# Later pairs' q and k by way of DRAM scratch, transposed as float32r, and the order ranked anew

## Chip, core and metric

The kernel runs on one core of a Trainium2 chip. The metric is the device time of one execution in microseconds (us), smaller is better. TensorE (PE, with its weight loads as PEld), VectorE (DVE), ScalarE (ACT), GpSimd (POOL) and SyncE (SP, which here only issues DMAs) each work through an instruction list of their own in order and meet at semaphores. TensorE multiplies a moving operand with a stationary one, which a weight load has put into the array before, and writes to PSUM. A tile is a buffer in SBUF or PSUM, the two memories on the chip.

## The reference

Attention with a compressive memory over 4 batches of 8 heads (576 tokens, width 64), then two feed-forward blocks on its output as 2304 tokens of width 512:

```python
scores = scale * np.matmul(q, k.transpose(0, 1, 3, 2))      # causal mask, softmax -> a
local = np.matmul(a, v)
q_p = phi(q)                                                # elu(q) + 1
mem_out = einsum(q_p, M_prev) / (einsum(q_p, z_prev) + 1e-6)
x = g * mem_out + (1 - g) * local                           # g = sigmoid(beta), per head
r = np.maximum(x @ w_in, 0.0)                               # 512 -> 2048
x = (s * (r * r) + b) @ w_out                               # 2048 -> 512
out = (sigmoid(x @ w_gate) * (x @ w_val)) @ w_out2          # 512 -> 1536 -> 512
```

## The kernel before

**Stages.** The 32 heads are taken as 16 pairs of heads, numbered j = 0 to 15, four to a batch. Attention fills about the first 390 us. The product with w_in (tiles `h`, line 338; 128 chunks of twelve multiplications, `h_2_0_5` is chunk 5 of the first window of batch 2) can begin for a batch when its four pairs are done, and its chunks stand between the attention of the following pairs. Then come y (the product with w_out, line 1555, which reads r back from DRAM), the products m with w_gate and w_val (line 1874) and o with w_out2 (line 2008).

**A pair.** q and k come in as [128 tokens, 5 blocks, 2 x 64] (`rawq`, `rawk`, two buffers each). Both are needed with the width on the partitions, so TensorE turns each of the five 128x128 blocks: `transposed` (line 467) makes a block the stationary operand and multiplies it with an identity matrix (tiles `qt`, `kt`). ScalarE and VectorE write the result to SBUF as two float32r tiles, a rounded part and its rest (`QT`, `KT`). Next come scores (`sc`), softmax (VectorE's `nm`, ScalarE's exponentials `P`), turned probabilities (`pt`), and the product with v (`acc`). The first batch's four pairs (`DIRECT`, j = 0 to 3) take another way with float32 products (`o`, `ret`, `xt`), the twelve later ones keep all products in float32r. In the later pairs GpSimd normalises the probabilities (line 778) before they are turned, and `ft` turns phi(q). The profile prints f32 for float32r operands of TensorE too; which they are is seen in the code: `KT`, `QT`, `PTB`, `PT_A`, `VHL`, `x`, `w_in` are float32r, `rawq`, `rawk`, `ident`, `phi` and `P` are float32.

**Order.** A planner (`Plan`) writes every engine's list. Each step has an engine, a cost, an urgency worked out from the table `TUNE`, and what it reads, writes and needs as buffers; `order` simulates them and takes the most urgent step that is ready. The table and the costs thus change nothing but the order; on the chip every list is followed as it stands, on SP too.

## Time and profile before

| | |
|---|---|
| median of 3 runs | 1046.77 us (1042.32 to 1053.78) |
| the profiled execution | 1041.78 us, of which its span (first to last instruction) is 1040.0 us |
| granted TensorE clock, mean of the span | 0.997 |
| TensorE busy | 1018.5 us, 98% |
| VectorE, ScalarE, GpSimd busy | 827.9, 602.4, 174.0 us |
| DMA | 230.60 MB, mean 222 GB/s |

Busy times of TensorE count a multiplication from its start to its modelled end, and neighbours overlap. So what a multiplication takes from TensorE's time is read from the distance of two starts, not from its own length, and a wait is read where the timeline names a releaser.

### The profile page before, as it was taken

How to read it: one execution, taken by the hardware profiler on the slowest of the kernel's cores; microseconds unless marked ns; L12 is line 12 of the kernel's file. 1: busy time of each engine (PE TensorE's matmuls, PEld its weight loads, DVE VectorE, ACT ScalarE, POOL GpSimd, SP SyncE). 2: the span in 40 equal slices, each digit the busy share in tenths (PEclk: the TensorE clock that was granted, in tenths of full speed). 3: DMA queues.
4: the chain of work that ended last, by engine and by line, in shares of the span. 5: the costliest groups of instructions: out<-in, count | busy, mean ns of one | idle time of the engine just before them, and what ended most of it. 6: DMA issues, size and time to landing. Idle time of an engine off the chain costs nothing.

```text
span 1040.0 us, 20327 instructions
## 1 busy us (share of the span) xinstructions
PE 1018.5 (98%) x7182; PEld 991.5 (95%) x7182; DVE 827.9 (80%) x1760; ACT 602.4 (58%) x1322; POOL 174.0 (17%) x258
## 2 busy tenths in 40 slices
PE   6999999999999999999999999999999999999998
PEld 4888999999999999999999999999999999999998
DVE  5888888987887766788998884878968779677775
ACT  5778787877787667666877674223531226322243
POOL 2345655444444420000000000000000000000000
PEclk9999999999999999999999999999999999999999
DMA  6634454344534239877989988777797778877774
GB/s 139 152 101 114 138 144 131 100 127 119 147 116 129 92 135 337 286 253 278 324 290 364 375 301 300 248 254 253 265 347 256 254 257 263 282 267 251 253 268 157
DMA packets 182885, 230.60 MB, mean 222 GB/s; under 512 B 71936, under 2 KB 136960, under 8 KB 182784
## 3 DMA queue, kind: packets, MB, share of 16 engines
q1 hardware_dynamic: 181136, 228.48, 67.2%
q8 instruction: 57, 0.93, 0.4%
q10 hardware_dynamic: 1648, 0.82, 0.3%
q14 instruction: 44, 0.36, 0.1%
HBM read 171.06 MB, written 58.20 MB: 220 GB/s over the span
## 4 chain that ended last, share of the span: by engine, by line
PE 95%; DMA 1%; DVE 1%; ACT 1%; issue 1%; SPq 0%; POOL 0%; ACTq 0%; DVEq 0%; POOLq 0%
PE m L1874 25%; PE y L1555 19%; PE h L338 19%; PE o L2008 13%; PE sc L720 3%; PE acc L904 2%; PE o L1283 2%; PE acc L905 2%; PE pt_B L851 1%; PE sc L746 1%; PE acc L908 1%; PE pt_D L851 1%; PE pt_A L851 1%; PE sc L1150 1%; PE ft L467 1%; PE qt L467 1%
## 5 line engine op out<-in xcount | busy, mean ns | idle before, releaser
L1874 PE MATMUL m<-yt,ws 128*128 128x384 f32 x1512 | 262.6, 335 | 0.0
L1874 PEld LDWEIGHTS m<-yt,ws 128*128 128x128 f32 x1512 | 262.0, 188 | 0.0
L338 PE MATMUL h<-x,w_in 128*128 128x256 f32 (+1 forms) x1536 | 224.7, 300 | 2.1 <-ACT r L348 2.0
L338 PEld LDWEIGHTS h<-x,w_in 128*128 128x128 f32 x1536 | 209.2, 190 | 5.2 <-ACT r L348 2.7
L1886 DVE TENSOR_TENSOR set<-m,set 128x384 f32<-128x384 f32 x252 | 132.6, 553 | 53.4 <-PE m L1874 47.8
L1555 PE MATMUL y<-gh,w_out 128*128 128x384 f32 (+1 forms) x768 | 150.5, 338 | 0.0
L1555 PEld LDWEIGHTS y<-gh,w_out 128*128 128x128 f32 x768 | 135.5, 188 | 0.0
L2008 PE MATMUL o<-wo,ps 128*128 128x256 f32 x1134 | 134.0, 280 | 0.0
L2008 PEld LDWEIGHTS o<-wo,ps 128*128 128x128 f32 x1134 | 133.9, 188 | 0.0
L1890 ACT ACTIVATE set<-set 128x384 f32<-128x384 f32 x72 | 37.9, 526 | 84.6 <-DVE set L1886 84.6
L348 ACT ACTIVATE r<-h 128x320 f32<-128x320 f32 (+1 forms) x128 | 52.0, 410 | 57.3 <-PE h L338 51.3
L1555 PE MATMUL y<-gl,w_out 128*128 128x384 f32 x384 | 83.0, 337 | 0.0
L1990 ACT CAST ps<-p 128x384 fp32r<-128x384 f32 x72 | 36.9, 513 | 68.7 <-PE o L2008 35.1
L700 DVE CUSTOM_DVE_ANT_0 P<-sc,mask 128x256 f32<-128x256 f32 (+4 forms) x144 | 68.1, 514 | 8.2 <-PE sc L720 5.6
L1555 PEld LDWEIGHTS y<-gl,w_out 128*128 128x128 f32 x384 | 68.6, 188 | 0.0
L778 POOL TENSOR_SCALAR P<-P,rs 128x384 f32<-128x384 f32 (+4 forms) x108 | 64.5, 618 | 20.2 <-DVE rs L774 17.1
L762 ACT ACTIVATE P<-P,nm 128x384 f32<-128x384 f32 (+4 forms) x108 | 62.4, 580 | 9.1 <-DVE nm L700 8.7
L1540 DVE TENSOR_TENSOR gl<-rr,gh 128x384 fp32r<-128x384 f32 x96 | 52.6, 555 | 14.1 <-PE y L1555 6.7
L1535 ACT CAST gh<-rr 128x384 fp32r<-128x384 f32 (+1 forms) x96 | 49.1, 512 | 18.7 <-PE y L1555 14.6
L1882 ACT COPY set<-m 128x384 f32<-128x384 f32 x36 | 17.4, 482 | 72.0 <-PE m L1874 72.0
L1531 ACT ACTIVATE rr<-rr 128x384 f32<-128x384 f32 (+1 forms) x96 | 49.0, 521 | 3.0 <-DMA rr<-relu_scratch 2.8
L1994 DVE TENSOR_TENSOR ps<-p,ps 128x384 fp32r<-128x384 f32 x72 | 39.8, 555 | 11.4 <-ACT ps L1990 9.9
(194 smaller groups left out, 1583.9 us busy)
## 6 DMA issues: line engine op xcount, KB each, us to landing
ws<-weight_scratch SPq DMA_DIRECT2D x108, 512.0 KB, 4.6
wo<-out_weight_scratch SPq DMA_DIRECT2D x63, 512.0 KB, 4.3
rr<-relu_scratch SPq DMA_DIRECT2D x96, 192.0 KB, 5.0
weight_scratch<-wp SPq DMA_DIRECT2D x36, 512.0 KB, 5.5
out_weight_scratch<-ov_h SPq DMA_DIRECT2D x42, 256.0 KB, 3.4
relu_scratch<-r SPq DMA_DIRECT2D x32, 320.0 KB, 2.6
ws<-weight_scratch SPq DMA_DIRECT2D x36, 256.0 KB, 3.2
raw_w_in<-in_moe_w_in_dram SPq DMA_DIRECT2D x16, 512.0 KB, 4.4
```

Of the source, the lines that this page charges most:

```text
L338: nc.tensor.matmul(t[:, :n], wt[:, wi, c], x[:, xi, c], start=(m == 0), stop=(m == 3 * NK - 1))
L348: nc.scalar.activation(rts[b, c0, f - f % 2][:, f % 2, :n], t[:, :n], AF.Relu)
L700: nc.vector.tensor_tensor_reduce(out=pr, in0=ps, in1=mk, scale=1.0, scalar=3e38, op0=ALU.add, op1=ALU.min, accum_out=nm,)
L762: nc.scalar.activation(pr, pr, AF.Exp, bias=T.pop(("nm", j, e, t)), scale=-1.0, accum_out=T["sums", j][:, col : col + 1],)
L778: nc.gpsimd.tensor_scalar(out=pr, in0=pr, scalar1=T["rs", j, part][:, n : n + 1], scalar2=1.0, op0=ALU.mult, op1=ALU.mult,)
L1531: nc.scalar.activation(r_sb[step], r_sb[step], AF.Square)
L1535: nc.scalar.copy(gh, r_sb[step])
L1540: nc.vector.tensor_tensor(out=gl, in0=r_sb.pop(step)[:, :n], in1=gs[step][0][:, :n].bitcast(F32), op=ALU.subtract,)
L1555: nc.tensor.matmul(accs[wi][d][:, : y.shape[1]], w_out_sb[f][:, x, d], y, start=(f == 0 and x == 0 and y is gh), stop=(f == NF - 1 and y i ...
L1874: nc.tensor.matmul(acc, wt[:, a, k : k + P], yt[:, y, c], start=(m == 0), stop=(m == 3 * K2 - 1),)
L1886: nc.vector.tensor_tensor(out=t[:, o], in0=Z["m", z, x], in1=t[:, i], op=ALU.add)
L2008: nc.tensor.matmul(Z["zo", pi, x, i][:, c * C : (c + 1) * C], ps[:, a, r * P : (r + 1) * P], wt[:, y * C : (y + 1) * C], start=(f == 0 and ...
```

## The change

Four things are changed. For the twelve later pairs, SP first copies the pair's q and k, DRAM to DRAM, into scratch tensors of its own (`copy`: 24 copies of 288 KB), and the loads read the scratch. The tiles they fill are float32r (written through a float32 view, so that the words are not converted), and `transposed` then multiplies with an identity of type float32r. The first four pairs keep float32. The identity is made in a buffer of another tile and copied over by GpSimd. The planner reckons 58 ns in place of 112 ns for a block in all `qt` and `kt`, gets the 24 copies as steps, and has a new table, so the order of nearly everything up to the end of the attention is another; from the last chunks of `h` to the end TensorE's list is the same instruction by instruction.

```diff
--- before.py
+++ after.py
-    "mem": -104539.7, "lq": 25883.4, "lk": -1533.8, "lv": 53002.6, "lm": 1567.6, "q": -1758.6,
...
+    "mem": -106340.2, "lq": 27443.5, "lk": -1029.3, "lv": 41230.5, "lm": 1427.5, "q": -1937.4,
...
+    qs_d = dram("q_scratch", [B, H, S, D])
+    ks_d = dram("k_scratch", [B, H, S, D])
...
-    ident = const.tile([P, P], F32, name="ident")
-    nc.gpsimd.memset(ident, 0.0)
+    identr = const.tile([P, P], F32R, name="identr")
+    ident = identr.bitcast(F32)
+    eye = stage.tile([P, NK * P], F32, tag="f", name="eye", bufs=FB)[:, :P]
...
+    nc.gpsimd.tensor_copy(identr, eye)
...
-    rawqs = [at.tile([P, NQ, P], F32, name=f"rawq{i}", bufs=1) for i in range(2)]
-    rawks = [at.tile([P, NQ, P], F32, name=f"rawk{i}", bufs=1) for i in range(2)]
     rawv = at.tile([P, NQ, P], F32, name="rawv", bufs=1)
+    raws = {}
+
+    def raw_of(c, j):
+        return raws[c, j % 2, j in DIRECT]
+
+    def make_raw(j):
+        for c in "qk":
+            t = raws[c, j % 2, j in DIRECT] = at.tile(
+                [P, NQ, P], F32 if j in DIRECT else F32R, tag=f"raw{c}{j % 2}", name=f"raw{c}{j}",
+                bufs=1,
+            )
+            t = t if j in DIRECT else t.bitcast(F32)
+            if c == "k":
+                nc.gpsimd.memset(t[LAST:, NQ - 1], 0.0)
+                continue
+            for e in range(2):
+                r = slice(e * LAST, (e + 1) * LAST)
+                nc.gpsimd.memset(t[r, NQ - 1, (1 - e) * D : (2 - e) * D], 0.0)
...
+        from_q, from_k = src is q, src is k
+        if from_q or from_k:
+            dst = raw_of("q" if from_q else "k", j)
+            if j not in DIRECT:
+                dst, src = dst.bitcast(F32), qs_d if from_q else ks_d
...
+    def copy(j, src):
+        b, p = jobs[j][:2]
+        h = slice(2 * p, 2 * p + 2)
+        nc.sync.dma_start((qs_d if src is q else ks_d)[b, h], src[b, h])
...
-            nc.tensor.transpose(o, src[:, i], ident)
+            if src.dtype == F32R:
+                nc.tensor.transpose(o.bitcast(F32R), src[:, i], identr)
+            else:
+                nc.tensor.transpose(o, src[:, i], ident)
...
+            bounce = not direct and src is not v
+            if bounce:
+                add(
+                    "SP", 450, lambda src=src: copy(j, src), u + du + AT["cp"],
+                    reads=[("ld", j - 2)], writes=[(key + "d", j)], late=2300, size=3e5,
+                )
             add(
                 "ACT" if src is q and j == 0 else "SP", 600 * ne,
                 lambda src=src, dst=dst, ta=ta: load_raw(j, src, dst, ta), u + du,
-                new=[(key, (key, j))], late=2300, size=(t1 - ta) * P * (500 if direct else 800),
+                reads=[(key + "d", j)] if bounce else [],
+                writes=([(key, j)] if first and src is not v else []) + ([("ld", j)] if src is k else []),
+                new=[] if first and src is not v else [(key, (key, j))], late=2300, size=(t1 - ta) * P * (500 if direct else 800),
...
-        add("PE", flip(nt), qt, u + AT["q"], reads=[("rawq", j)],
+        add("PE", 58 * nt + 30, qt, u + AT["q"], reads=[("rawq", j)],
```

The start of the program on SP, before and changed (`raw_w_in` is a part of w_in, `mem` of M_prev and z_prev; the number behind a name is the pair, or the part of w_in):

```order
L410 DMA rawk0_93<-in_k_dram 128x4x64 x2
L421 DMA rawk0_93<-in_k_dram 64x2x64
L410 DMA rawk1_94<-in_k_dram 128x4x64 x2
L421 DMA rawk1_94<-in_k_dram 64x2x64
L251 DMA raw_w_in0_136<-in_moe_w_in_dram 128x4x256
L251 DMA raw_w_in1_142<-in_moe_w_in_dram 128x4x256
L448 DMA mem0_147<-in_M_prev_dram 128x64
L449 DMA mem0_147<-in_z_prev_dram 128x1
```

```order
L256 DMA raw_w_in0_111<-in_moe_w_in_dram 128x4x256
L256 DMA raw_w_in1_114<-in_moe_w_in_dram 128x4x256
L473 DMA mem0_117<-in_M_prev_dram 128x64
L474 DMA mem0_117<-in_z_prev_dram 128x1
L430 DMA rawk0_102<-in_k_dram 128x4x64 x2
L441 DMA rawk0_102<-in_k_dram 64x2x64
L430 DMA rawk1_107<-in_k_dram 128x4x64 x2
L441 DMA rawk1_107<-in_k_dram 64x2x64
```

The first two parts of w_in and pair 0's memory now stand ahead of k of pairs 0 and 1.

The start of the program on TensorE, before and changed:

```order
L467 MATMUL kt0_154<-ident_64,rawk0_93 128x128 x5
L467 MATMUL qt0_0_167<-ident_64,rawq0_91 128x128 x4
L467 MATMUL qt0_4_172<-ident_64,rawq0_91 128x128
L467 MATMUL kt1_188<-ident_64,rawk1_94 128x128 x5
L1150 MATMUL sc0_0_0_203<-KT0_165,QT0_185 128x128
L1150 MATMUL sc0_1_0_204<-KT0_165,QT0_185 128x128
...
L1095 MATMUL ret0_0_229<-mem0_147,phi0_194 128x65
```

```order
L495 MATMUL qt0_0_180<-identr_64,rawq0_99 128x128 x4
L495 MATMUL qt0_4_185<-identr_64,rawq0_99 128x128
L495 MATMUL kt0_190<-identr_64,rawk0_102 128x128 x5
L1138 MATMUL ret0_0_226<-mem0_117,phi0_203 128x65
L1138 MATMUL ret0_1_227<-mem0_117,phi0_203 128x65
...
L1144 MATMUL ret0_0_226<-mem0_117,phi0_203 64x65 x2
L495 MATMUL kt1_241<-identr_64,rawk1_107 128x128 x5
L1193 MATMUL sc0_0_0_258<-KT0_210,QT0_196 128x128
L1193 MATMUL sc0_1_0_259<-KT0_210,QT0_196 128x128
```

The scores of pair 0 (`sc0`) now stand behind its memory product (`ret0`), and q's transposes ahead of k's.

TensorE where pair 4 follows pair 3, before and changed (`qt6` and `ft4` are transposes of pairs 6 and 4, `xt3` turns pair 3's output, `pt4_B0` and `pt4_A0` turn normalised probabilities of pair 4):

```order
L467 MATMUL qt6_1321<-ident_64,rawq0_91 128x128 x5
L1317 MATMUL xt3_1_1348<-ident_64,X3_1_1309 128x128 x2
L1324 MATMUL xt3_1_1348<-ident_64,X3_1_1309 64x64 x2
L467 MATMUL ft4_1357<-ident_64,phi4_1037 128x128 x5
L338 MATMUL h_0_256_0_1375<-x0_256_770,w_in0_138 128x320 x12
L851 MATMUL pt4_A0_1398<-ident_64,P4_0_0_1318 128x128
L851 MATMUL pt4_A0_1398<-ident_64,P4_0_1_1328 128x128 x2
L851 MATMUL pt4_B0_1402<-ident_64,P4_4_1288 128x128
L851 MATMUL pt4_B0_1402<-ident_64,P4_0_2_1223 128x128
```

```order
L493 MATMUL qt6_1367<-identr_64,rawq4_505 128x128 x5
L1360 MATMUL xt3_1_1395<-identr_64,X3_1_1361 128x128 x2
L1367 MATMUL xt3_1_1395<-identr_64,X3_1_1361 64x64 x2
L495 MATMUL ft4_1402<-identr_64,phi4_1015 128x128 x5
L894 MATMUL pt4_B0_1428<-identr_64,P4_4_1339 128x128
L894 MATMUL pt4_B0_1428<-identr_64,P4_0_2_1291 128x128
L894 MATMUL pt4_B0_1428<-identr_64,P4_0_3_1322 128x128
...
L894 MATMUL pt4_A0_1457<-identr_64,P4_0_0_1374 128x128
L894 MATMUL pt4_A0_1457<-identr_64,P4_0_1_1377 128x128 x2
L343 MATMUL h_0_256_0_1465<-x0_256_836,w_in0_113 128x320 x12
```

The chunk of `h` that stood between `ft4` and the first `pt4` now stands behind all of them.

TensorE at the end of the attention, before and changed (`acc15_0_1` is the last product that x of the first window of batch 3, `x3_0`, waits for):

```order
L338 MATMUL h_2_256_15_5760<-x2_256_4548,w_in15_2315 128x320 x12
L904 MATMUL acc15_0_1_5778<-PT15_A1_5758,VHL15_5229 128x256
...
L908 MATMUL acc15_0_1_5778<-FS15_1_5596,mst15_5222 128x256
L851 MATMUL pt15_D1_5785<-ident_64,P15_1_3_5536 128x128
...
L904 MATMUL acc15_1_0_5789<-PTB15_5691,VHL15_5229 128x320
...
L908 MATMUL acc15_1_0_5789<-FS15_0_5595,mst15_5222 128x320
L904 MATMUL acc15_1_1_5807<-PTB15_5691,VHL15_5229 128x320
...
L338 MATMUL h_3_0_0_5825<-x3_0_5805,w_in0_138 128x256 x12
```

```order
L343 MATMUL h_2_256_15_5789<-x2_256_4685,w_in15_2017 128x320 x12
L947 MATMUL acc15_0_0_5809<-PT15_A0_5786,VHL15_5341 128x256
...
L894 MATMUL pt15_D1_5839<-identr_64,P15_1_3_5648 128x128
...
L947 MATMUL acc15_1_0_5844<-PTB15_5775,VHL15_5341 128x320
...
L951 MATMUL acc15_1_0_5844<-FS15_0_5751,mst15_5332 128x320
L947 MATMUL acc15_0_1_5861<-PT15_A1_5836,VHL15_5341 128x256
...
L951 MATMUL acc15_0_1_5861<-FS15_1_5752,mst15_5332 128x256
L947 MATMUL acc15_1_1_5870<-PTB15_5775,VHL15_5341 128x320
...
L343 MATMUL h_3_0_0_5895<-x3_0_5886,w_in0_113 128x256 x12
```

`acc15_0_1` is moved behind `acc15_1_0`, so that only `acc15_1_1` stands between it and the chunk `h_3_0_0`, which reads `x3_0`.

## Rows read from the trace of the kernel before

**Rows 1.** The page: busy us by engine (share of the span, instructions), and the chain.
```profile
PE 1018.5 (98%) x7182; PEld 991.5 (95%) x7182; DVE 827.9 (80%) x1760; ACT 602.4 (58%) x1322; POOL 174.0 (17%) x258
...
PE 95%; DMA 1%; DVE 1%; ACT 1%; issue 1%; SPq 0%; POOL 0%; ACTq 0%; DVEq 0%; POOLq 0%
```

**Rows 2.** One stretch: us, busy us by engine (instructions), granted clock, DMA share, GB/s.
```profile
320.00:360.00 40.00, 40.00 (x310) 38.02 (x309) 31.33 (x74) 27.38 (x70) 14.65 (x18) 1.00 0.33 109
```

**Rows 3.** Group of TensorE multiplications: count, busy us, mean ns, idle before.
```profile
L467 PE MATMUL kt<-ident,rawk 128*128 128x128 f32 x80 | 12.7, 294 | 6.0 <-DMA rawk<-in_k_dram 5.5 <-DVE KT L1072 0.5
```

**Rows 4.** Groups of TensorE weight loads (PEld), columns as in rows 3.
```profile
L904 PEld LDWEIGHTS acc<-PTB,VHL 128*128 128x128 f32 x96 | 18.1, 188 | 2.8 <-DVE nm L700 0.7 <-issue 0.6
...
L905 PEld LDWEIGHTS acc<-PTB,VHL 128*64 128x64 f32 x96 | 13.1, 136 | 0.0
...
L467 PEld LDWEIGHTS kt<-ident,rawk 128*128 128x128 f32 x80 | 9.8, 150 | 7.0 <-POOL vals L440 5.5 <-DVE KT L1072 0.9 <-PE pt_A L851 0.3
```

**Rows 5.** Timeline: first and fifth transpose of a later pair's k (start, us, engine, line).
```profile
321.71 0.27 PE L467 MATMUL kt<-ident,rawk 128*128 128x128 f32 x1
...
322.14 0.27 PE L467 MATMUL kt<-ident,rawk 128*128 128x128 f32 x1
```

**Rows 6.** Timeline, three products of a later pair, one behind the other on TensorE.
```profile
207.42 0.22 PE L904 MATMUL acc<-PT_A,VHL 128*128 128x128 f32 x1
207.48 0.22 PE L905 MATMUL acc<-PT_A,VHL 128*64 128x128 f32 x1
...
207.54 0.33 PE L908 MATMUL acc<-FS,mst 128*128 128x256 f32 x1
```

**Rows 7.** Timeline of the first 27 us, TensorE and ScalarE.
```profile
5.48 1.34 PE L467 MATMUL kt<-ident,rawk 128*128 128x128 f32 x5 [5.48 <-DMA rawk<-in_k_dram]
...
9.61 1.65 PE L1150 MATMUL sc<-KT,QT 64*128 64x128 f32 x12
...
10.33 0.68 ACT L269 ACTIVATE f_w_in<-raw_w_in 128x512 f32<-128x512 f32 x1
...
17.21 0.48 ACT L1260 COPY PT_A<-pt_A 128x384 f32<-128x384 f32 x1 [4.32 <-PE pt_A L1243]
...
26.25 1.23 ACT L287 CAST w_in<-raw_w_in 128x512 fp32r<-128x512 f32 x2
```

**Rows 8.** Waits of TensorE, the second to fifth longest of 13: total us, times, longest.
```profile
PE h L338 <- ACT r L348: 2.0, 1, 2.0
PE xt L1317 <- POOL X L1309: 1.7, 1, 1.7
PE pt_C L1243 <- ACT P L1190: 1.4, 1, 1.4
PE ret L1095 <- DMA mem<-in_z_prev_dram: 1.2, 1, 1.2
```

**Rows 9.** Timeline at 91 us, GpSimd and TensorE, where pair 4 follows pair 3.
```profile
91.25 4.80 POOL L778 TENSOR_SCALAR P<-P,rs 128x384 f32<-128x384 f32 x9 [0.39 <-DVE rs L774]
...
92.07 3.06 PE L338 MATMUL h<-x,w_in 128*128 128x320 f32 x12
```

**Rows 10.** Group of GpSimd: normalisation of one block of probabilities, 512 columns.
```profile
L778 POOL TENSOR_SCALAR P<-P,rs 128x512 f32<-128x512 f32 x24 | 17.8, 741 | 0.0
```

**Rows 11.** Timeline at 381 us, from the attention's last products to h.
```profile
380.87 0.37 ACT L928 COPY XB<-acc 64x256 f32<-64x256 f32 x1
...
382.29 0.31 PE L904 MATMUL acc<-PTB,VHL 128*128 128x320 f32 x1
...
382.80 1.22 DVE L996 TENSOR_TENSOR x<-XB,x 128x1024 fp32r<-128x1024 f32 x1 [0.66 <-ACT x L992]
...
383.69 2.57 PE L338 MATMUL h<-x,w_in 128*128 128x256 f32 x18
```

**Rows 12.** DMA issues: out<-in, engine, count, KB each, median us to landing.
```profile
ws<-weight_scratch SPq DMA_DIRECT2D x108, 512.0 KB, 4.6
...
rawk<-in_k_dram SPq DMA_DIRECT2D x32, 128.0 KB, 3.0
```

More of the change, by code (lines that the diff above doesn't have):

```diff
@@ L209, in attention_moe_kernel @@
     w1 = w1s.enter_context(tc.tile_pool(name="w1", bufs=16, side="left"))
-    ident = const.tile([P, P], F32, name="ident")
-    nc.gpsimd.memset(ident, 0.0)
+    identr = const.tile([P, P], F32R, name="identr")
+    ident = identr.bitcast(F32)
+    eye = stage.tile([P, NK * P], F32, tag="f", name="eye", bufs=FB)[:, :P]
+    nc.gpsimd.memset(eye, 0.0)
     nc.gpsimd.affine_select(
-        out=ident, in_=ident, compare_op=ALU.not_equal, fill=1.0, base=0,
+        out=eye, in_=eye, compare_op=ALU.not_equal, fill=1.0, base=0,
         pattern=[[-1, P]], channel_multiplier=1,
     )
+    nc.gpsimd.tensor_copy(identr, eye)
     gt = const.tile([P, H], F32, name="gt")
@@ L355, in h_store @@
         )
-    rawqs = [at.tile([P, NQ, P], F32, name=f"rawq{i}", bufs=1) for i in range(2)]
-    rawks = [at.tile([P, NQ, P], F32, name=f"rawk{i}", bufs=1) for i in range(2)]
     rawv = at.tile([P, NQ, P], F32, name="rawv", bufs=1)
-    def zero_raw():
-        for t in rawks:
-            nc.gpsimd.memset(t[LAST:, NQ - 1], 0.0)
-        for t in rawqs:
-            for e in range(2):
-                nc.gpsimd.memset(t[e * LAST : (e + 1) * LAST, NQ - 1, (1 - e) * D : (2 - e) * D], 0.0)
+    raws = {}
[14 more added lines that the diff above has]
+                nc.gpsimd.memset(t[r, NQ - 1, (1 - e) * D : (2 - e) * D], 0.0)
+    def zero_raw():
+        make_raw(0)
+        make_raw(1)
         nc.gpsimd.memset(rawv[: P - LAST, NQ - 1], 0.0)
@@ L413, in load_raw @@
             )
-        if t1 == NQ and src is q:
+        if t1 == NQ and from_q:
             for e in range(2):
@@ L419, in load_raw @@
         elif t1 == NQ:
-            lo = 0 if src is k else P - LAST
+            lo = 0 if from_k else P - LAST
             eng.dma_start(
@@ L529, in plan_load @@
         direct = j in DIRECT
+        first = j in (0, 1, NP, NP + 1)
+        if j in (NP, NP + 1):
+            add("POOL", 900, lambda: make_raw(j), u + AT["lq"] - 20,
+                new=[("rawq", ("rawq", j)), ("rawk", ("rawk", j))])
+        elif first:
+            add("BAR", 0, lambda: None, -1000, reads=[("zero", 0)],
+                new=[("rawq", ("rawq", j)), ("rawk", ("rawk", j))], late=0)
         for src, dst, ta, key, du in (
-            (q, rawqs[j % 2], t0, "rawq", AT["lq"]), (k, rawks[j % 2], 0, "rawk", AT["lk"]),
+            (q, None, t0, "rawq", AT["lq"]), (k, None, 0, "rawk", AT["lk"]),
             (v, rawv, 0, "rawv", AT["lv"]),
@@ L563, in qt @@
         def qt():
-            T["qt", j] = transposed(rawqs[j % 2], t0, t1, f"qt{j}")
+            T["qt", j] = transposed(raw_of("q", j), t0, t1, f"qt{j}")
         def q_hi():
@@ L583, in kt @@
         def kt():
-            T["kt", j] = transposed(rawks[j % 2], 0, t1, f"kt{j}")[:, :nk]
+            T["kt", j] = transposed(raw_of("k", j), 0, t1, f"kt{j}")[:, :nk]
         def k_hi():
@@ L594, in k_lo @@
             )
-        add("PE", flip(t1), kt, u + AT["k"], reads=[("rawk", j)],
+        add("PE", 58 * t1 + 30, kt, u + AT["k"], reads=[("rawk", j)],
             new=[(bank(t1), ("kt", j)), ("KT", ("KT", j))], late=250)
@@ L607, in phi_a @@
             nc.scalar.activation(
-                flat(), rawqs[j % 2][:, t0:t1].rearrange("p t d -> p (t d)"), AF.Relu, scale=-1.0
+                flat(), raw_of("q", j)[:, t0:t1].rearrange("p t d -> p (t d)").bitcast(F32), AF.Relu, scale=-1.0
             )
@@ L613, in phi_b @@
             nc.vector.scalar_tensor_tensor(
-                out=flat(), in0=rawqs[j % 2][:, t0:t1].rearrange("p t d -> p (t d)"), scalar=0.0,
+                out=flat(), in0=raw_of("q", j)[:, t0:t1].rearrange("p t d -> p (t d)").bitcast(F32), scalar=0.0,
                 in1=flat(), op0=ALU.max, op1=ALU.add,
@@ L1017, in qt @@
             T["qt", j] = [
-                (slice(a * P, c * P), transposed(rawqs[j % 2], a, c, f"qt{j}_{a}", True)) for a, c in parts
+                (slice(a * P, c * P), transposed(raw_of("q", j), a, c, f"qt{j}_{a}", True)) for a, c in parts
             ]
@@ L1063, in kt @@
         def kt():
-            T["kt", j] = transposed(rawks[j % 2], 0, t1, f"kt{j}", True)[:, :nk]
+            T["kt", j] = transposed(raw_of("k", j), 0, t1, f"kt{j}", True)[:, :nk]
         def k_hi():
@@ L2110, in attention_moe_kernel @@
     AT = TUNE
+    add("POOL", 1500, zero_raw, -1000, writes=[("zero", 0)])
     add("ACT", 500, load_consts, AT["lc"], writes=[("gates", 0)], late=2300, size=4e3)
```

1 line of the change is left out of this document (removed), and 14 rows, old and new, of the table TUNE.

## Prediction

> **What bounds the kernel now.** I read the page's busy table and its chain first. TensorE is busy for 1018.5 of 1040.0 us, and the chain that ended last lies on it for 95%; no other engine has more than 1% of that chain [rows 1]. The one-stretch view says the same of the middle of the attention: in 320 to 360 us TensorE works all 40 us, and the DMA engines stand at a share of 0.33 [rows 2]. So a nanosecond of TensorE saved there counts nearly whole, provided that its list has something ready to move up. In the attention that something is `h`: its chunks stand between the steps of every pair from the fifth on. A nanosecond taken from another engine counts nothing, except where TensorE is seen to wait. TensorE's waits are few. The longest is the first one, 5.5 us for k of pair 0 [rows 3], and the next four are 2.0, 1.7, 1.4 and 1.2 us long, each once [rows 8]. From the last chunks of `h` on, TensorE's order is unchanged, so whatever is won or lost by then is carried to the end.
>
> **Term 1, the transposes.** The first of five transposes of a later pair's k begins at 321.71 and the fifth at 322.14 us [rows 5]: four distances in 0.43 us, 0.108 us each. What would they take as float32r? The nearest rows are products with a float32r moving operand of 128 columns, as the identity will be: they begin at 207.42, 207.48 and the next at 207.54 us, 60 ns apart [rows 6]. TensorE has 80 such products for all `kt`, five in each of 16 pairs [rows 3], and as many for `qt`; the twelve later pairs have 120 of the 160. So 120 x (108 - 60) ns = 5.8 us. The other end is nothing: what may hold a row of transposes back is the weight load, because each transpose loads a block of its own. A float32r load of 128 columns stands in the trace with 188 ns and one of 64 columns with 136 ns, while the float32 blocks of k took 150 ns [rows 4]. The 64 columns more cost 52 ns, and if they cost that in every row, 128 columns take 104 ns, and a chain of float32r transposes keeps the distance that it has. Against it: between 207.42 and 207.54 us the loads of 64 and of 128 columns both went in, in 0.12 us [rows 6], where that price gives 156 ns. I take -5.8, with 0 as the other end.
>
> The Trainium skill has a rule that speaks against the change: its page "TensorE: Matmul & The Clock Gate", section "LDWEIGHTS (loading the stationary operand)", puts a load at its columns over 1.2 in ns, whatever else, which is 107 ns for 128 columns, an estimate almost equal to the present distance; by it term 1 would be about 0. The trace disagrees for pairs of loads (0.12 us where the rule gives 160 ns) [rows 6], so I give it no more than the chance of its rival below. The same page's section "Weight-path perf modes" says that a faster load is taken for 128 weights whose type is not FP32; float32r's longer load rows [rows 4] do not show it.
>
> **Term 2, the start.** Two parts of w_in, 512 KB each, and pair 0's memory now stand ahead of k on SP. On ScalarE two passes over w_in and one cast stand ahead of the evictions of `qt0`, 0.68 + 0.68 us and half of 1.23 us [rows 7], 2.0 us. On TensorE `sc0`, twelve products in 1.65 us, and pair 1's `kt`, 1.34 us like the first one [rows 7], leave the place where they ran beside the wait for the memory and go behind it. If none of that is made good, it costs 1.65 + 1.34 = 3.0 us. For it speaks that this work has to be done at some time: today the cast stands at 26.25 us, in the way of pair 0's softmax, ScalarE has 4.32 us idle before 17.21 us [rows 7], and TensorE waits 1.4 us for P and 1.2 us for the memory [rows 8], which now lands earlier. If both waits go, and half of the idle time is put to use besides, about 2 us are won on balance. I take +0.5, near the middle, with -2 and +3 as ends.
>
> **Term 3, pair 3 to pair 4.** Today a chunk of `h` of 3.06 us begins right behind `ft4` at 92.07 us [rows 9] and gives GpSimd time to normalise pair 4's probabilities. In the changed list `pt4_B0` stands right behind `ft4` and needs three normalised blocks. GpSimd begins them at 91.25 us [rows 9], at up to 0.74 us a block [rows 10]: 91.25 + 2.2 = 93.4 us against 92.07, a new wait of 1.3 us. It is nothing if GpSimd begins earlier by as much, and at most the 3.06 us that the chunk has covered. I take +1.3, ends 0 and +3.
>
> **Term 4, the end of the attention.** `x3_0` needs `acc15_0_1`. From its first eviction at 380.87 us to the end of the last step on VectorE, at 382.80 + 1.22 = 384.02 us, it takes 3.15 us [rows 11]. In the changed list only `acc15_1_1` and the first two products of `h_3_0_0` (which read the half of x that is ready sooner) stand in between: 383.69 - 382.29 = 1.4 us for the one [rows 11] and, by 2.57 us for 18 products, 2 x 0.14 us for the others. That leaves 1.5 us of waiting. Today a later chunk of the same batch waits 2.0 us for ScalarE's r [rows 8]; a delay ahead of it shortens that wait, and I credit somewhat more than half. So +0.6, ends 0 and +1.5.
>
> **Parts taken at nothing.** The 24 copies of 288 KB lie between the 128 KB loads, 3.0 us from issue to landing, and the 512 KB ones, 4.6 us [rows 12]. In the changed SP list a copy stands some fifteen entries or more ahead of the load that reads it; DMA engines at a share of 0.33 [rows 2] can take what is added. If a copy came late, the load would stop SP, and with it the stores of r behind it: that is the third rival. The identity's way by a second buffer, and its copy on GpSimd, lie beside the first wait of 5.5 us [rows 3]. The planner's lower cost is only an order, in the terms above.
>
> **The sum.** -5.8 + 0.5 + 1.3 + 0.6 = -3.4 us. The profiled execution took 1041.78 us, 1.8 us more than its span of 1040.0, so it would take 1038.4. The median of the three runs shown is 5.0 us above the profiled one, and the same sum from there is 1046.77 - 3.4 = 1043.4. I predict 1043 us. With every end against the forecast but term 1's the sum is -5.8 + 3 + 3 + 1.5 = +1.7 (1048.5), with every end for it -5.8 - 2 = -7.8 (1039.0).
>
> **Rivals.** *The transposes don't get faster.* The load of a new block every time sets the pace at 104 ns, as the 52 ns for 64 columns say [rows 4]. Then only the new waits are left, +2.4 us, 1049.2. For it: those load rows, longer for float32r than for float32. Against it: the distances of 60 ns [rows 6].
>
> *The order wins too.* The new table removes waits that I leave in place: the four of 2.0, 1.7, 1.4 and 1.2 us make 6.3 us [rows 8]. If they go, and the new places cost nothing, -5.8 - 6.3 = -12.1 us, 1034.7. For it: nearly everything ahead of 390 us is ordered afresh. Against it: in the two places that I followed I count new waits.
>
> *Slower: the copies hold up SP.* Every entry of SP's list waits for those ahead of it. If a copy lands later than the entries between it and its load have been issued, the load stops the list, stores of r stand, the buffers of r stay full, and the next chunk of `h` cannot be evicted. By the 18 products in 2.57 us [rows 11] a chunk of twelve takes 1.7 us; one lost in each of the twelve later pairs is 20.6 us, and with the sum of -3.4 it gives +17.2, 1064. It decides once a copy takes several times the 4.6 us of a 512 KB transfer [rows 12]. Against it: the DMA share of 0.33 [rows 2], and that the copies run about two pairs ahead.
>
> **How the numbers follow.** My forecast has a chance of 0.59, the unchanged transposes 0.20, the better order 0.13, the held-up SP 0.08. A change of 1% (10.5 us) is about what a measurement of this kernel can tell from no change. Faster by over 1% is below 1036.3: the better order and little else, 0.15. Slower by over 1% is above 1057.2: the held-up SP, 0.08. The rest, 0.77, is within 1%. The range of 1034 to 1051 takes in the forecast's ends (1039.0 to 1048.5), the unchanged transposes (1049.2) and the better order (1034.7), and leaves out the held-up SP and some of the spread of the runs.
>
> **What would show it.** The distances of `kt` and `qt` transposes in later pairs: 60 ns right, 104 or more wrong. In the timeline: the start of the first `sc` (9.61 us before [rows 7]); the wait of `pt_B` for GpSimd near 92 us, 1.3 us; the wait of `h` for VectorE's x near 382 us, 1.5 us. In the view of waits no raw load of a later pair should hold TensorE, and SP should show no long stop at one. The prediction is wrong if TensorE's waits sum to much more or less than before, or if the float32r distance sits between 60 and 104 ns.

## The result and the profile after

The changed kernel takes 1057.69 us (median of 11 runs, 1055.73 to 1061.67), the kernel before 1044.13 us (11 runs, 1040.49 to 1054.17): a ratio of 1.013, 95% interval 1.0106 to 1.0155, slower by 1.1 to 1.6%. The profiled execution took 1057.04 us with a span of 1055.2, 15.2 us more than before. Medians take all runs, the ratios are those of the record and no quotients of the medians; some runs of the kernel before take about 1054 us at a mean clock of 0.985, three of the 17 timed beside e13 and none of the 13 beside e5.

The table says where the time went. It compares when TensorE begins the same piece of work in the two timelines. Since the order is another, not the same work lies ahead of every row (71 multiplications ahead of `kt` of pair 2 before, 100 after); ahead of `h_3_0_0` it is the same 3000 in both.

| TensorE begins | before, us | after, us | late by |
|---|---|---|---|
| first transpose | 5.48 | 9.15 | 3.7 |
| `kt` of pair 2 | 19.1 | 32.5 | 13.4 |
| `kt` of pair 3 | 41.4 | 53.3 | 11.9 |
| first `h` | 74.8 | 87.9 | 13.1 |
| first `h` of batch 3 (`h_3_0_0`) | 383.7 | 395.7 | 12.0 |
| last product of `h` | 468.9 | 483.8 | 14.9 |
| last product of `o` | 1035.1 | 1050.4 | 15.3 |

So 11 to 12 us are lost by 41 us of the kernel before (its 250th multiplication begins 10.9 us later in the changed one), nothing on balance from there to the end of the attention, and 3 more between there and the last `h`. The timeline of the start, TensorE, then ScalarE, then SP, answers to [rows 7]:

```profile
9.15 1.30 PE L495 MATMUL qt<-identr,rawq 128*128 128x128 f32 x5 [9.15 <-DMA rawq<-in_q_dram]
...
16.82 2.36 PE L1193 MATMUL sc<-KT,QT 64*128 64x128 f32 x18
...
23.66 1.09 PE L1286 MATMUL pt_A<-identr,P 128*128 128x128 f32 x3 [3.49 <-ACT P L1233]
...
33.63 2.66 PE L1326 MATMUL o<-vals,PT_A 128*128 128x65 f32 x12
```
```profile
22.66 0.66 ACT L274 ACTIVATE f_w_in<-raw_w_in 128x512 f32<-128x512 f32 x1 [5.08 <-DMA raw_w_in<-in_moe_w_in_dram]
```
```profile
6.11 2.84 SPq L430 DMA_DIRECT2D rawk<-in_k_dram  x2
...
17.88 0.54 SPq L256 DMA_DIRECT2D raw_w_in<-in_moe_w_in_dram  x1
...
24.28 0.59 SPq L449 DMA_DIRECT2D k_scratch<-in_k_dram  x1
...
28.11 0.55 SPq L449 DMA_DIRECT2D q_scratch<-in_q_dram  x1
28.70 1.86 SPq L430 DMA_DIRECT2D vals<-in_v_dram  x2
```

k's first load is issued at 6.11 us (0.73 before) behind w_in and the memory. The four loads ahead of it take SP only 1.9 us to issue; for 3.5 us SP stands until loads issued earlier have landed, and 1.6 us more between the two halves of k. Its waits up to 31 us, the first three of four:

```profile
SPq L474 <- DMA gt<-in_beta_dram: 2.1, 1, 2.1
SPq L430 <- DMA rawq<-in_q_dram: 1.6, 1, 1.6
SPq L430 <- DMA raw_w_in<-in_moe_w_in_dram: 1.4, 1, 1.4
```

Up to pair 0's v the loads and copies take SP as long to issue as before (its issues add up to 21.0 and 20.9 us), and v is issued 3.2 us later all the same. Scores begin at 16.82 us in place of 9.61 [rows 7]. Then ScalarE stands 5.08 us: its list has the third part of w_in ahead of pair 0's exponentials, SP issued that part only at 17.88, and TensorE waits 3.49 us for `P`. The windows of the start (columns as in [rows 2]) show TensorE nearly empty from 20 to 24 us at a DMA share of 0.97, then busy at half clock (0.50 is the lower of the two levels, 1.2 GHz):

```profile
20.00:24.00 4.00, 0.51 (x3) 0.18 (x1) 1.03 (x5) 1.34 (x4) 0.00 (x0) 0.77 0.97 271
24.00:28.00 4.00, 4.00 (x17) 2.87 (x17) 1.93 (x7) 3.33 (x8) 0.00 (x0) 0.50 0.96 244
```

The same view over the whole stretch up to `h_3_0_0` tells waits from clock; the lines are of the kernel before, of the changed one and of e5 (an experiment below):

```profile
0.00:383.69 383.69, 368.85 (x3001) 342.37 (x3001) 306.57 (x764) 288.21 (x690) 172.28 (x242) 1.00 0.45 127
0.00:395.71 395.71, 374.68 (x3001) 350.04 (x3001) 308.97 (x779) 289.46 (x697) 177.56 (x249) 0.96 0.49 144
0.00:392.18 392.18, 371.37 (x3000) 345.53 (x3001) 309.84 (x779) 289.86 (x697) 178.39 (x249) 0.99 0.50 145
```

TensorE is busy for 368.85 of 383.69 us before and for 374.68 of 395.71 us after, so it is idle for 14.8 and 21.0 us: 6 of the 12 us are waits. In the other 6 the same multiplications take longer. Behind its first rise (ahead of that the clock has no record, see e5) the clock is at half for some 31 us in the changed kernel (22 to 29, 32 to 43, 77 to 84 and 104 to 111 us) and for 3 us before (93 to 96).

The waits of TensorE, answering to [rows 8]:

```profile
PE qt L495 <- DMA rawq<-in_q_dram: 9.2, 1, 9.2
PE pt_A L1286 <- ACT P L1233: 3.5, 1, 3.5
PE h L343 <- ACT r L353: 2.3, 2, 1.7
...
PE pt_B L894 <- POOL P L821: 1.0, 1, 1.0
PE h L343 <- DVE x L1039: 0.8, 1, 0.8
PE h L343 <- ACT x L1035: 0.7, 1, 0.7
```

Later pairs' transposes, answering to [rows 5] and [rows 4], the timeline's first and fifth of a group and the group of weight loads from 50 to 400 us:

```profile
131.52 0.22 PE L493 MATMUL qt<-identr,rawq 128*128 128x128 f32 x1
131.81 0.25 PE L493 MATMUL qt<-identr,rawq 128*128 128x128 f32 x1
```
```profile
L493 PEld LDWEIGHTS kt<-identr,rawk 128*128 128x128 f32 x60 | 6.2, 144 | 0.3 <-issue 0.3
```

Four distances in 0.29 us here, against 0.43 before; this group is a short one, the median of the 24 groups of later pairs is 0.37 us against 0.44. The third and fourth distance are 86 and 85 ns at the median (109 ns before), the second is 65 ns, and the first as long as before (118 ns, 110 before). The transposes are faster, and the kernel is slower.

### The profile page after: what moved, and what is told of

It reads as the page before. It is cut to its first block, busy times and chain, and to the rows that moved or that the text cites. A ratio compares the mean times of both kernels' runs of the same rounds, so it can differ in the third digit from the quotient of the medians.

```text
span 1055.2 us, 20385 instructions
## 1 busy us (share of the span) xinstructions
PE 1026.5 (97%) x7182; PEld 1000.7 (95%) x7182; DVE 825.1 (78%) x1760; ACT 601.2 (57%) x1322; POOL 179.5 (17%) x265
## 4 chain that ended last, share of the span: by engine, by line
PE 93%; DVE 2%; ACT 1%; DMA 1%; SPq 1%; issue 1%; POOL 0%; ACTq 0%; DVEq 0%; POOLq 0%
PE m L1917 25%; PE h L343 19%; PE y L1598 18%; PE o L2051 13%; PE sc L763 3%; PE o L1326 2%; PE acc L947 2%; PE acc L948 2%; PE pt_B L894 1%; PE sc L789 1%; PE acc L951 1%; PE sc L1193 1%; PE pt_A L894 1%; PE pt_D L894 1%; DMA rawq<-in_q_dram 1%
## 5 line engine op out<-in xcount | busy, mean ns | idle before, releaser
L821 POOL TENSOR_SCALAR P<-P,rs 128x384 f32<-128x384 f32 (+4 forms) x108 | 67.3, 643 | 43.4 <-DVE rs L817 34.5
L1578 ACT CAST gh<-rr 128x384 fp32r<-128x384 f32 (+1 forms) x96 | 49.2, 513 | 27.6 <-PE y L1598 20.9
```

The costliest lines, as they stand in the source:

```text
L821: nc.gpsimd.tensor_scalar(out=pr, in0=pr, scalar1=T["rs", j, part][:, n : n + 1], scalar2=1.0, op0=ALU.mult, op1=ALU.mult,)
L1578: nc.scalar.copy(gh, r_sb[step])
```

## The experiments

Each was timed beside the kernel before. Late by `h_3_0_0` is read from its profiled execution as in the table.

### The copies alone

**The kernel before with 24 copies on SP** (e6), nothing in float32r, no new order:

```diff
...
+        if src is k and j + 2 < NJ and j + 2 not in DIRECT:
+            b, p = jobs[j + 2][:2]
+            h = slice(2 * p, 2 * p + 2)
+            nc.sync.dma_start(ks_d[b, h], k[b, h])
+            nc.sync.dma_start(qs_d[b, h], q[b, h])
```

> The kernel before with nothing but the 24 copies added on SP, at the places that they have in e4_words; nothing reads the scratch, loads and transposes stay as before. Theory 6 (SP issues without a pause from 1 to 35 us, each copy takes 0.6 us of it, six stand ahead of pair 0's v; TensorE then waits 3.9 us, its clock falls to half, and the work up to 41 us runs at half): about 1057 us, the 1055.7 of e4_words plus the 2 us that float32r saved there. Theory 7 (the loss in e4_words comes from the loads out of scratch or the float32r tiles): 1043 to 1045.

1055.0 us, ratio 1.011 (1.0087 to 1.0133). In the old order the copies alone cost nearly what the whole change costs. SP's timeline, TensorE's, and the windows:

```profile
12.14 0.57 SPq L430 DMA_DIRECT2D k_scratch<-in_k_dram  x1
12.76 0.59 SPq L431 DMA_DIRECT2D q_scratch<-in_q_dram  x1
...
28.82 0.60 SPq L430 DMA_DIRECT2D k_scratch<-in_k_dram  x1
29.46 0.59 SPq L431 DMA_DIRECT2D q_scratch<-in_q_dram  x1
30.09 1.13 SPq L412 DMA_DIRECT2D vals<-in_v_dram  x2
```
```profile
28.97 0.77 PE L1250 MATMUL pt_D<-ident,P 128*128 128x128 f32 x5
34.28 2.79 PE L1290 MATMUL o<-vals,PT_A 128*128 128x65 f32 x12 [4.54 <-DMA vals<-in_v_dram]
```
```profile
32.00:36.00 4.00, 1.72 (x8) 1.75 (x9) 0.00 (x0) 0.00 (x0) 0.00 (x0) 0.75 0.67 149
36.00:40.00 4.00, 4.00 (x22) 4.00 (x22) 1.24 (x5) 0.97 (x2) 0.73 (x1) 0.50 0.69 154
40.00:44.00 4.00, 4.00 (x29) 3.43 (x28) 0.77 (x4) 0.50 (x2) 0.00 (x0) 0.50 0.81 256
```

Each copy takes SP 0.6 us to issue. Six of them (three pairs like these) stand ahead of pair 0's v, whose load is issued at 30.09 us; before, SP's timeline has it 4.5 us earlier (in the changed kernel only two copies stand ahead of it):

```profile
25.55 1.14 SPq L410 DMA_DIRECT2D vals<-in_v_dram  x2
```

TensorE waits 4.54 us for it, and its clock falls to half and stays there while it is busy. `kt` of pair 3 begins at 53.67 us, 12.3 late, and `h_3_0_0` 12.1 late: nothing more is lost in between.

**The same with TensorE kept busy in that wait** (e9), by transposes of the identity whose result is overwritten:

```diff
+                for i in range(40 if (j, win) == (0, 0) else 0):
+                    nc.tensor.transpose(o[:, i % 4 * P : (i % 4 + 1) * P], ident, ident)
```

> e6_copies (the kernel before with 24 idle copies on SP) with 40 extra transposes of the identity on TensorE right ahead of pair 0's first product with v, where it waits 4.5 us: 4.4 us of work at full clock, into the tile that the product then overwrites. Nothing comes earlier by it. Theory A (the wait costs 4.5 us and the fall of the clock behind it 6 to 7 us more): TensorE stays busy, the clock stays, 1055 - 6.5 = 1048.5 us. Theory B (the whole loss of e6_copies comes from late data): 1055, or more by what the extra work overruns.

1048.97 us, 1.0034 (1.0009 to 1.006): 6 us less than e6 with the same late v. Here the clock is back at full while the added transposes run:

```profile
28.00:32.00 4.00, 4.00 (x24) 3.75 (x21) 2.44 (x11) 2.51 (x6) 2.58 (x2) 0.58 0.76 214
32.00:36.00 4.00, 4.00 (x39) 4.00 (x37) 0.00 (x0) 0.00 (x0) 0.00 (x0) 1.00 0.72 162
```

So in the old order late data costs 4 to 5 us and the half clock behind it some 6.

**Old order, copies on SP, float32r words** (e4): before's table and costs, the copies as in e6, raw tiles of pairs 4 to 15 and their transposes in float32r as in the changed kernel. **The same with the copies on GpSimd's queue** (e7), and **float32r only from pair 6 on, copies on SP only from pair 5's k load on** (e13, which leaves pairs 4 and 5 in float32); the edits of e7 and e13 against e4:

```diff
-            nc.sync.dma_start(ks_d[b, h], k[b, h])
+            nc.gpsimd.dma_start(ks_d[b, h], k[b, h])
```
```diff
-        direct = j < NP
+        direct = j < NP + 2
...
-        if from_k and j + 2 < NJ and j + 2 not in DIRECT:
+        for i in ((NP + 2, NP + 3) if j == NP + 1 else (j + 2,)) if from_k and NP < j < NJ - 2 else ():
```

> The kernel before, with its own table, costs and order on every engine, and only the words changed: later pairs' q and k are copied to scratch (two copies right behind the load of k two pairs earlier), loaded from there as float32r and transposed in float32r. Theory 1 (the transposes gain what their distances in the trace of the changed kernel say, about 84 ns in place of 109, 120 times): -3.0 us against before, 1041 us. Theory 3 (60 ns, as predicted, once the order is out of the way): -5.8, 1038. Theory 4 (the copies or the loads from scratch cost as much as the transposes win): 1044 or more.

> e4_words (the order of the kernel before, with float32r words by way of scratch), but GpSimd's queue issues the 24 copies in place of SP, at the same places of the program. The bytes and their time are the same; only SP's 0.6 us for each is gone. Theory 6 (SP's issue time is what the copies cost): pair 0's v comes as early as before, the clock stays, and what is left is the gain of the transposes, 1043 - 2 = 1041 us. Theory 8 (the copies' bytes crowd the loads of the start): still 1050 or more.

> The order of the kernel before, with float32r words by way of scratch for pairs 6 to 15 only; pairs 4 and 5 stay float32 without a copy, and the 20 copies go out on SP from pair 5's load of k on, when v of pairs 0 to 2 has been issued. Theory 6 (a copy costs only where SP issues without a pause, and every stall of some us at the start costs its clock as well; the transposes win about 0.10 us for each group of five): nothing is lost at the start, 20 groups win 2.1 us, 1044.2 - 2 = 1042 us. Theory 11 (what TensorE wins is waited away at the next operand from VectorE or ScalarE): 1044, no change.

e4: 1055.65 us, 1.0093 (1.0058 to 1.0128), missed: it waits 3.9 us for v like e6. e7: 1046.23, 1.0026 (1.0009 to 1.0042): with the copies off SP's list 9.4 us come back by the medians (7 by the ratios), though their bytes are the same, but the 1041 us hoped for are missed; its wait of `acc` for `PT_A` is longer (1.8 us, 0.6 before) and that of `o` for v (1.2) is new. The Trainium skill, "DMA: Bandwidth & Descriptors", section "Rules for kernel authors", says that spreading DMAs over the issuing engines brings no bandwidth and only saves issue time; e4 against e7 agrees on the issue time. e13: 1044.77 against 1043.19, ratio 0.9996 (0.9967 to 1.0025): without the loss at the start float32r gains nothing that can be measured. Its profile waits 2.6 us for `r` of ScalarE where before's waits 2.0 [rows 8].

### Float32 words in the changed kernel

**The changed kernel, loads and order kept, later pairs' raw tiles in float32 again** (e5):

```diff
-                [P, NQ, P], F32 if j in DIRECT else F32R, tag=f"raw{c}{j % 2}", name=f"raw{c}{j}",
+                [P, NQ, P], F32, tag=f"raw{c}{j % 2}", name=f"raw{c}{j}",
...
```

> The changed kernel with later pairs' q and k as float32 again: the copies, the loads from scratch and the whole order stay, only the tiles and the transposes are float32 as before. Theory 1 (float32r saves about 25 ns in each of 120 transposes): 3 us slower than the changed kernel, 1060.7. Theory 3 (48 ns, as predicted): 1063.5. Theory 5 (float32r gains nothing where it counts): 1057.7.

1056.45 us, 1.0117 (1.0102 to 1.0133): not slower than with float32r, and the 1060.7 us expected of a gain of 25 ns a block are missed. But the clock is not the same in the two (mean 0.989 to 0.996 in e5's runs, 0.981 to 0.987 in those of the changed kernel). The lists are the same, so the two can be laid side by side: from the 129th product of `h` to `h_3_0_0` the changed kernel takes 395.71 - 136.44 = 259.27 us, e5 392.18 - 131.43 = 260.75. Float32r saves 1.5 us there, with the clock at full in both. Ahead of that stretch e5 is 5.0 us earlier, with waits as long (20.8 us idle up to `h_3_0_0`, above). What differs is the clock, and its column must be read with care at the start:

```profile
24.00:28.00 4.00, 4.00 (x17) 2.70 (x18) 1.93 (x7) 3.50 (x8) 0.00 (x0) 1.00 0.97 246
```
```profile
27.75 1.27 PE L494 MATMUL qt<-identr,rawq 128*128 128x128 f32 x5
...
36.34 0.71 PE L494 MATMUL qt<-identr,rawq 128*128 128x128 f32 x5
```

The column says 1.00 at 24 to 28 us, yet five transposes take 1.27 us there, as long as those of the changed kernel at half clock (1.27 us at 27.59), and 0.71 us later. The column has nothing ahead of the clock's first rise (in the kernel before too, five transposes at 6.62 us take 1.28 us). By these lengths e5's clock rises only near 30 us, but then stays at full up to 98 us, where the changed kernel falls to half twice. So e5 is 8.5 us late at `h_3_0_0` with half clock up to 30 us, the changed kernel 12.0 us late with half clock at 32 to 43 and 77 to 84 us besides.

### Which part of the start

**The kernel before with only SP's first entries in the changed order** (e15), w_in, w_in and pair 0's memory (steps 78, 84 and 14 of the plan) ahead of k:

```diff
+        for n in (14, 84, 78):
+            steps.remove(n)
+            steps.insert(0, n)
```

> Only the first entries of SP's list are changed in the kernel before: two parts of w_in and pair 0's memory stand ahead of k of pairs 0 and 1, as in the changed kernel; every other list is as before. Theory S (the order on SP makes the loss at the start): the first transposes begin near 9 us in place of 5.5, everything behind is late by 4 us or more and the clock falls once more on the way, so 1044 + 5 to 12, about 1052. Rival theory O (the order on TensorE and ScalarE makes it, and SP's order is made good by the next waits): 1044 to 1046.

1047.17 us against 1044.06, 1.0018 (0.9991 to 1.0046), nearer to theory O. The first transpose begins at 11.11 us, 5.6 late; the wait for the memory is gone, and at the first `pt_A` (16.33 us before) 2.3 are left. SP stands as in the changed kernel (2.0 us for `gt`, 1.6 for q, 1.5 for w_in), and pair 0's v is issued 3.3 us late; `h_3_0_0` is 2.7 late. The order on SP alone is worth about 3 us, which the interval does not tell from nothing.

**The changed kernel with the copies on GpSimd's queue** (e16), its lists otherwise the same:

```diff
-        nc.sync.dma_start((qs_d if src is q else ks_d)[b, h], src[b, h])
+        nc.gpsimd.dma_start((qs_d if src is q else ks_d)[b, h], src[b, h])
```

> The changed kernel with its 24 copies issued on GpSimd's queue in place of SP's, the lists otherwise the same. Theory S (of the changed kernel's loss at the start the six early copies carry little, since k, w_in's conversion and P are late ahead of them): 1055 to 1058. Rival theory D (the copies carry as much here as in the old order, some 9 us): about 1048.

1061.82 us, 1.016 (1.0092 to 1.0227), worse than either theory. GpSimd issues the first four copies at 14.8 to 16.5 us (SP at 24.3 to 34.6), beside the loads of the start: ScalarE waits for w_in's third part until later,

```profile
26.71 0.66 ACT L274 ACTIVATE f_w_in<-raw_w_in 128x512 f32<-128x512 f32 x1 [9.17 <-DMA raw_w_in<-in_moe_w_in_dram]
```

9.17 in place of 5.08 us, and TensorE waits 6.57 us for `P`. By the lengths of its transposes the clock rises near 34 us in this execution (five take 1.27 us at 31.64 us, 0.77 at 36.53) and stays at full to 100 us; TensorE begins `kt` of pair 3 at 53.53 us, as late as in the changed kernel (53.26), and `h_3_0_0` 12.6 us late. Longer waits and less time at half clock come out even.

**Waits of the changed kernel moved or filled.** e2 puts the conversion of w_in's third part (steps 119 to 123 of the planned list) behind pair 0's `P`. e3 puts 30 transposes of the identity into the wait for `P`; e14 has these and another 16 ahead of the first `o`. (`move` takes the steps named out of the planned list and puts them behind the last one named.)

```diff
+        move([119, 120, 121, 122, 123], 231)
```
```diff
+            if (j, g) == (0, "A0"):
+                for i in range(30):
+                    nc.tensor.transpose(ps[:, i % 3 * P : (i % 3 + 1) * P], ident, ident)
...
+                for i in range(16 if (j, win) == (0, 0) else 0):
+                    nc.tensor.transpose(o[:, i % 4 * P : (i % 4 + 1) * P], ident, ident)
```

> The changed kernel, in which only the conversion of w_in's part 2 (one step on ScalarE, two on VectorE, and the two behind them) is moved behind pair 0's exponentials; loads stay. It takes away ScalarE's wait of 5.1 us for that part's load ahead of the first exponentials, and with it TensorE's wait of 3.5 us. Theory 1a (the wait also lets TensorE's clock fall to half, and some 8 us of work behind it run at half speed): 3.5 + about 4 = 7.5 us come back, 1050. Theory 1b (the clock would have been low anyway): 3.5 us, 1054. Theory 2 (waits later take it up): 0 to 2 us, 1056.

> The changed kernel with 30 extra transposes of the identity in TensorE's list right ahead of pair 0's first turned probabilities (they write the same PSUM tile, which is overwritten): 3.2 us of work at full clock, in a wait of 3.5 us. The wait itself stays; only TensorE is busy in it. Theory 1a (the fall of the clock in that wait costs about 4 us by itself): 1053.5 us. Theory 1b (the clock doesn't matter): 1057.7, or up to 2 us slower where the extra work runs at half clock and lasts beyond the wait.

> The changed kernel with extra transposes of the identity in both long waits of its start: 30 ahead of pair 0's first turned probabilities, 16 ahead of its first product with v. No data come earlier; only the clock should stay up between 20 and 42 us. Theory A (the changed kernel loses 4 to 5 us to the half clock of 22 to 42 us, besides what comes late): 1057.7 - 4 = 1053.5 us. Theory B (the late data alone set the time there, as e3_filler's median suggests): 1057.5.

1057.63 us (1.0107, 1.0023 to 1.0192), 1057.75 (1.0103, 1.0031 to 1.0175) and 1057.52 (1.0111, 1.0057 to 1.0166): none gains on the changed kernel. In e2 the wait for `P` is gone and `o` waits for v instead, 3.2 us; it begins at 33.52 us in place of 33.63. The profiled e3, the quickest of its four runs at 1054.86 us, has TensorE's clock at 1.00 from 24 to 32 us, 0.83 from 30 to 40, and is 7.6 us late at `h_3_0_0`; e14's falls later, to 0.70 and 0.62 in 70 to 90 us. What was gained is partly given back at the turn from `h` to y. TensorE in e2:

```profile
491.12 1.66 PE L1598 MATMUL y<-gh,w_out 128*128 128x384 f32 x8 [0.41 <-ACT gh L1578]
494.03 0.96 PE L1598 MATMUL y<-gl,w_out 128*128 128x384 f32 x4 [1.25 <-DVE gl L1583]
```

and in the changed kernel, without a wait:

```profile
494.00 0.98 PE L1598 MATMUL y<-gl,w_out 128*128 128x384 f32 x4
```

e2 ends `h` 1.9 us earlier and has lost it at 494.03. ScalarE there stands for a store of r (until 487.54 us in e2, 487.51 in the changed kernel), and VectorE's `gl` comes behind it.

**Hand-mended starts.** e1: k loaded first, w_in's parts behind it and their conversions behind the softmax. e8: the copies on GpSimd, v's load ahead, and e2's move.

```diff
+        move([15], 12)
+        move([106, 112], 18)
+        move([118, 124], 20)
+        move([107, 108, 109, 110, 111, 113, 114, 115, 116, 117], 231)
+        move([119, 120, 121, 122, 123], 342)
```
```diff
+        move([14], 17)
+        move([20], 22)
+        move([119, 120, 121, 122, 123], 231)
```

> The changed kernel, in which only the start is put back by hand: SP loads k of pair 0, its memory and k of pair 1 ahead of the first two parts of w_in, parts 2 and 3 of w_in later, and the conversion steps of parts 0 to 2 on ScalarE, VectorE and GpSimd stand behind pair 0's softmax. All the rest of the order, the copies and the float32r transposes stay. Theory 1 (the loss is made in the first 41 us: the trace of the changed kernel is 3.7 us late at the first transposes, 11.9 us late at pair 3's k, and still 12.0 late at h_3_0_0): about 11 us come back, 1046.5 us, between 1044 and 1049. Theory 2 (the new order has waits all along the attention, and a start that is earlier only waits there): under 4 us come back, 1054 or more.

> The changed kernel with three edits of its start and all the rest of its order kept: the copies are issued by GpSimd's queue, v of pairs 0 and 1 is loaded ahead of w_in's part 3 and of k of pair 3, and the conversion of w_in's part 2 stands behind pair 0's exponentials. By theory 6 there are two stalls of over 3 us in the changed kernel's start, each of which lets the clock fall, so that taking one away (e2_fwin2) only brought up the other; without both, 3.5 us of waiting and most of the half-clock stretch of 24 to 42 us come back: 1057.7 - 10 = 1048 us, between 1045 and 1050. Theory 2 (waits all along the attention take it up): 1055 or more.

Both missed: 1062.56 (1.0161, 1.0085 to 1.0237) and 1062.09 (1.0179, 1.0164 to 1.0195). TensorE's longest waits, e1 (behind its first, 6.1 us) and then e8:

```profile
PE pt_A L1286 <- DVE rm L1157: 5.8, 1, 5.8
PE o L1326 <- POOL w_in L295: 3.2, 1, 3.2
```
```profile
PE qt L495 <- DMA rawq<-in_q_dram: 15.1, 2, 9.6
```

Moving one load forward makes another late (pair 1's q in e8, 5.5 of the 15.1 us); e1's new waits are for VectorE and GpSimd. Of the cause they tell nothing apart.

**Planned anew.** Why does SP begin with w_in? In the changed plan the loads of pairs 0 and 1 read the step that zeroes the raw tiles; planned with before's table, it still began with w_in. e10 takes that dependence away, e11 also plans and issues the copies on GpSimd:

```diff
...
-        first = j in (0, 1, NP, NP + 1)
+        first = j in (NP, NP + 1)
...
-        elif first:
-            add("BAR", 0, lambda: None, -1000, reads=[("zero", 0)],
-                new=[("rawq", ("rawq", j)), ("rawk", ("rawk", j))], late=0)
```
```diff
-                    "SP", 450, lambda src=src: copy(j, src), u + du + AT["cp"],
+                    "POOL", 450, lambda src=src: copy(j, src), u + du + AT["cp"],
```

> The changed kernel with its table, costs and copies, but without one new dependence in its plan: loads of pairs 0 and 1 no longer wait for the planned 1.5 us of GpSimd's zeroing (as in the kernel before). The plan then puts k of pairs 0 and 1 first on SP again, ahead of w_in; other steps move with it. Theory 9 (that dependence, not the table, made the late start; four copies still stand ahead of pair 0's v and cost 2.4 us on SP): first transposes at 5.5 us in place of 9.15, 1046 us where the clock stays and 1051 where it falls. Theory 10 (the table's order is bad all along): 1055 or more.

> e10_free with the copies as steps of GpSimd, in the plan and on the chip, so that nothing new stands ahead of v of pairs 0 and 1. Theories 6 and 9 together (start dependence and SP's issue time are the loss; what is left is the transposes' gain of about 2.5 us on TensorE and the waits that the new order makes at pair 4 and at the end of the attention, 2 to 4 us): 1043 us, between 1041 and 1046. Theory 10: 1050 or more.

e10: 1079.69 us, 1.0332 (1.026 to 1.0404). e11: 1057.07, 1.0122 (1.0063 to 1.018). k is first again (first transposes at 5.5 and 5.7 us), but the planner then orders everything afresh and new waits appear elsewhere: 7.0 us of `h` for VectorE's x in e10; in e11, 2 to 4 us late up to 283 us of the kernel before, 2.8 us of `qt` for `KT` near 298 us, with the clock at half from 298 to 305 us, 11 us late behind it. Neither tests the table by itself.

**A warm start of the kernel before** (e12): 17 identity transposes in the first wait.

```diff
+        for i in range(17 if name == "kt0" else 0):
+            nc.tensor.transpose(t[:, i % 4 * P : (i % 4 + 1) * P], ident, ident)
```

> The kernel before with 17 extra transposes of the identity ahead of pair 0's first ones, 3.6 us at the half clock of the start, in the 5.5 us in which TensorE waits for k. Theory A (the clock rises with work, here at 17.6 us, and the half clock until then costs TensorE's time): the clock is up some us earlier and 2 to 4 us are won, 1041 us. Theory C (up to there the loads and evictions set the pace): 1044, no change.

1044.74 us, 1.0015 (0.9984 to 1.0045): no change. In its profile pair 2's `kt` begins 1.0 us earlier (18.16 us), but the first `o` at 28.50 us in place of 28.21, when the first part of v has just landed as before. So up to there a faster TensorE gains nothing; this execution falls to half clock behind it (30 to 40 us), which the kernel before doesn't.

## Why the prediction was wrong

I predicted 1043 us, in 1034 to 1051; it is 1057.69. I forecast 3.4 us less than before, and it is 13.6 more (from the median of 11 runs before, 1044.13, my sum would have given 1040.7). By its own steps:

**Term 2 (the start, +0.5, ends -2 and +3) failed first.** Measured: 11 to 12 us by 41 us, copies included. I saw the order on SP and counted the work that it displaces. What it cost is waits and clock. The waits: 3.7 us until the first transpose, where SP stands for loads to land, and 3.49 for `P`; up to `h_3_0_0` TensorE is idle 6 us longer than before. The clock: it falls in the wait for `P` (at 22 us) and three times more, and multiplications that take longer are the rest of the 12 us; no term of mine had that. Alone, SP's order costs 3 us (e15), the end of my range; in the changed lists more is lost, since ScalarE's conversion of w_in's third part and then v (e2) are late as well. How much is clock, e5 shows: with the same lists and waits as long it is 3.5 us earlier at `h_3_0_0`, although its transposes are slower by 1.5 us, so the half clock that it is spared is worth some 5 us.

**"Parts taken at nothing" failed too.** I priced the copies by landing time and by a DMA share of 0.33 [rows 2], read at 320 us. What they use up is SP's time to issue, 0.6 us each, at the start, where SP's list is full up to 35 us. In the old order that alone costs 11 us (e6, with the half clock), and 9.4 of it leave with the copies' place on SP's list (e4 and e7). The third rival named the right queue and a wrong mechanism: nothing stops at a late copy and no chunk of `h` is lost per pair; v is issued late once. In the changed kernel the copies' share is not shown: only two stand ahead of pair 0's v, 1.1 us of issue, and with the copies off SP's list (e16) the third part of w_in comes later still.

**Term 1 (transposes, -5.8) had the way right and the size off.** 85 ns lies between the two ends, 60 and 104 ns; measured -1.5 us (e5, the stretch up to `h_3_0_0`) to -2.5 us (e7 against before, the 24 groups with their neighbours). The products 60 ns apart [rows 6] stood singly, with loads of 64 and 128 columns; in a row of transposes every load has 128, which may be why, but no run shows it. The Trainium skill, "TensorE: Matmul & The Clock Gate", section "Back-to-back issue gap", gives about 81 ns for a stream of pairs of load and product with 128 columns; the trace agrees with that (85), and not with the 107 ns of the page's rule for loads.

**Term 3 (+1.3) had the wait right**: `pt_B` waits 1.0 us for GpSimd (the clock is at half there, 0.51 in 104 to 108 us, which the term had not). **Term 4 (+0.6)** had the wait right, 0.65 + 0.76 = 1.4 us (1.5 predicted), and the credit wrong: the later waits for `r` did not shrink, 1.67 + 0.66 = 2.3 us against 2.0 [rows 8]. TensorE's clock also falls there:

```profile
395.71 0.50 PE L343 MATMUL h<-x,w_in 128*128 128x256 f32 x2 [0.65 <-ACT x L1035]
396.97 13.02 PE L343 MATMUL h<-x,w_in 128*128 128x256 f32 x94 [0.76 <-DVE x L1039]
411.65 1.70 PE L343 MATMUL h<-x,w_in 128*128 128x256 f32 x12 [1.67 <-ACT r L353]
```

(0.88 in 390 to 400 us, 0.95 in 400 to 410). `h_3_0_0` to the last `h` takes 88.1 us, 85.2 before: +2.9. With the 12 us of lateness at `h_3_0_0` this is nearly all of the 15.2 us of the span.

**Open.** What share of the 6 us of waits is SP's order and what share the copies in the changed kernel: the parts alone (3 and 11 us, with their clock) do not add up to it, and e2, e3, e14 and e16 only exchange one late load for another. Why e5, with the same lists, has its clock at half in other stretches is not shown. Which waits take back float32r's 2 us in e13 was not shown. The new table without the new dependence could not be had, since both come out of one plan.
